# Another hand-written order for the attention groups and the first expert's products of a fused kernel

## The chip, the cores and the metric

The kernel runs on one core of one Trainium2 chip. The metric is device time in microseconds, from launch to end, as a median of runs. The core has five engines with an instruction queue each: PE (matmuls; its weight loads are shown as PEld), DVE (vector), ACT (scalar and activations), POOL (GpSimd) and SP, which here only issues DMA transfers. Each engine works through its queue in order; what must wait for another engine waits on a semaphore, and everything queued behind it on that engine waits too.

## The reference

The program is a chain of three layers over 1152 tokens (2 batches of 576) of 512 features, all in 32-bit floats:

```
scores = q @ k.T / 8, masked (heads 0-3: a band of 32; heads 4-7: every 4th of 128)
attn   = exp(scores - max); attn /= sum(attn) + 1e-9;   x = attn @ v
out    = sum over 4 experts e of  p[:, e] * (relu(x @ w1[e]) @ w2[e])     # 512 -> 1024 -> 512
h      = out @ w_in;  g = h * sigmoid(1.702 * h);  result = g @ w_out     # 512 -> 2048 -> 512
```

Products of full 32-bit precision are made of three passes at a faster format: a number is split into a high part and a rest, and high*high, low*high and high*low are summed in PSUM.

## The kernel before

**Attention.** Only the blocks that the masks leave are computed. Heads go in four pairs; each of the two batches has for each pair a big part and a small part, 16 parts in all. A big part is two *groups*, a small part one, so there are 24 groups, numbered 0 to 23 in the order of the list `parts`: 0, 1 are pair 2 of batch 0; 2, 3 pair 3; 4, 5 pair 0; 6, 7 pair 1; 8 to 15 are the small parts of both batches; 16 to 23 the big parts of batch 1. Pairs 2 and 3 have the dilated mask and four tiles of scores to a group, pairs 0 and 1 the plain band and three (small groups three or four).

The steps of one group x have letters in the table that sets their order:

- `S x` the matmuls for the scores (PE; `S x y` takes two groups in turns), into one PSUM bank;
- `Q x` adds the mask and takes each row's minimum of the negated scores (DVE, one instruction per tile);
- then either `A x`, exponentials tile by tile, with the row's minimum as bias and the row sum as by-product (ACT), or `B x`, a subtraction of the minima from the whole group (POOL `p` or DVE `v`), `X x`, one exponential over the whole group (ACT), and `Y x`, the row sums (DVE);
- `N x` adds 1e-9 and takes the reciprocal (both DVE), then multiplies the group by it (POOL `p` or DVE `v`);
- `U x` transposes the group (PE, into a PSUM bank), `c x` copies it to SBUF (ACT `a`, DVE `v`);
- `V x` multiplies by the values once both groups of a part are there (PE, one bank); `C x` copies the result as the high part of the layer's input `xh`, `R x` forms the rest `xl` (DVE) and frees the bank.

**The first expert, expert 0.** Its tokens go in three chunks c of 384 and its hidden features in eight tiles f of 128. A first product (chunk c, tile f) is 12 matmuls: four slices of the input (one for each head pair) times three passes. Step `F it a b` does some of them for it = 8c + f: the terms a to b-1 of eight, of which 0 to 3 are the two passes with `xh` of slice 0 to 3, and 4 to 7 the one with `xl`. `G f i` does the same for chunk 0, tile f and slice `ORDER[i]`. `h it` (ACT, relu) and `l it` (DVE) read the bank and form the high and low part of the hidden tile; four such buffers go round. `2 it i` is the second product, three matmuls into the i-th of four long-lived banks; after tile 7 DVE multiplies each by the token's share and puts it into `acc`. `W s which` loads a weight slab of 512 KB into one of four staging buffers, `H` (ACT) and `O` (POOL or DVE) split it.

**Banks.** PSUM has eight banks here: four of the pool `ps`, which scores, transposes, value products and first products all take, and four of `pacc` for the second products (chunk 0's first products of tiles 0 to 2 borrow three of those before their time).

**What sets the order.** Up to chunk 1 the table `SCRIPT` is the program order of all five queues: a line of it is read step by step, and each step appends its instructions to its engines. Loads are steps of it too (`L` for q and k of a part, `K` for v, `W`), so it also sets the order of the transfers, all of them in one queue on SP. `P n` puts n matmuls on the constant 1.0 (`spin`), whose results nobody reads. Everything after the table (chunk 2, experts 1 to 3, the last layer) is written by other code:

```
for words_ in SCRIPT.split(","):
    what, *args_ = words_.split()
    steps[what](*(int(x) if x.lstrip("-").isdigit() else x for x in args_))
```

In names of rows, `s02big` is the bank of scores of batch 0, pair 2, big part; `prob`, `st` its exponentials and minima/sums, `ppt` and `pT` the transposed group in PSUM and SBUF, `pv` the value product, `g` (with expert, chunk and tile behind it) a first product, `pa` a second product, `h` the hidden tile, `st_`, `wh`, `wl` a staged slab and its two parts.

Of the kernel before, what the change touches and what calls it, by code (L numbers as in the profile page):

```python
# [76 lines left out]
F 0 7 8, H 1 0 1, Q 8, R 5, O 1 0 v 2, L 10, W 2 0, K 6, D, A 8, K 7, O 1 0 p 1, N 8 p, G 0 2 h, G 1 1 l, U 8, c 7 a,
Q 9, A 9, K 8, W 3 0, L 11, H 0 1 0, c 8 v, N 9 v, V 7, S 10, F 1 0 1, G 1 1 h, F 0 6 7, F 0 0 1, U 9, F 0 2 3, Q 10,
C 7 a, A 10, H 0 1 1, R 7, O 1 0 v 0, F 0 3 6, F 1 6 7, F 0 1 2, N 10 v, H 1 1 0, h 0, c 9 v, O 0 1 v 0, V 8, S 11,
C 8 v, S 12, F 1 7 8, V 9, F 1 3 4, F 1 2 3, Q 11, Q 12, A 12, A 11, l 0, O 0 1 v 1, F 1 5 6, R 8, F 1 4 5, O 1 0 p 3,  # L80
F 2 1 6, U 10, N 12 v, 2 0 0, F 2 0 1, F 1 1 2, O 0 1 v 2, c 10 a, K 9, L 12, L 13, K 10, N 11 p, U 11, H 1 1 1, h 1,
C 9 a, F 2 6 8, c 11 v, O 0 1 v 3, U 12, V 10, V 11, h 2, R 9, l 1, S 13, c 12 v, H 2 0 0, S 14, C 11 a, V 12, l 2,
R 11, O 2 0 p 0, Q 13, Q 14, H 3 0 0, C 12 a, 2 0 1, F 3 7 8, 2 1 0, 2 0 2, F 3 6 7, F 3 5 6, F 3 1 2, F 3 2 5, 2 0 3,
F 3 0 1, 2 1 1, H 2 0 1, A 14, C 10 a, R 12, O 1 1 p 1, O 1 1 v 0, O 2 0 p 1, O 2 0 p 2, A 13, K 11, W 3 1, W 2 1,
L 14, K 12, N 14 v, O 1 1 p 2, O 2 0 p 3, R 10, h 3, N 13 v, l 3, U 14, U 13, c 14 a, c 13 v, H 3 0 1, F 4 2 8, 2 1 2,
2 1 3, F 4 0 1, F 4 1 2, S 15, V 14, h 4, V 13, C 14 a, H 3 1 0, H 2 1 0, H 2 1 1, R 14, C 13 v, R 13, O 3 0 p 1,
O 1 1 v 3, O 3 0 p 2, O 2 1 p 2, O 2 1 p 3, Q 15, 2 2 0, H 3 1 1, B 15 v, X 15, Y 15, F 5 0 2, 2 2 1, 2 3 0, F 5 2 5,
F 5 5 8, 2 3 1, 2 2 2, 2 3 2, 2 2 3, O 3 0 p 3, l 4, N 15 v, h 5, K 13, O 2 1 v 1, l 5, O 3 1 p 2, O 3 0 p 0, L 15,
U 15, F 6 4 6, F 6 2 4, F 6 6 8, 2 3 3, F 6 0 2, w, c 15 a, V 15, h 6, S 16 17, l 6, Q 17, Q 16, C 15 a, B 16 v, R 15,
X 16, Y 16, O 2 1 p 0, O 3 1 p 0, O 3 1 p 1, B 17 v, X 17, Y 17, F 7 7 8, F 7 3 4, 2 4 0, F 7 2 3, F 7 5 6, F 7 6 7,  # L90
F 7 1 2, F 7 0 1, 2 4 1, 2 4 2, 2 5 0, 2 5 1, F 7 4 5, 2 5 2, h 7, Z, F 8 6 7, F 8 0 1, 2 4 3, F 8 1 2, N 16 p,
N 17 p, 2 6 0, U 16, F 8 2 6, K 14, 2 5 3, F 8 7 8, U 17, l 7, c 16 a, c 17 a, S 18 19, V 17, Q 19, Q 18, A 18,
C 17 a, h 8, R 17, A 19, N 18 p, l 8, 2 6 1, O 3 1 v 3, 2 7 0, F 10 0 6, F 9 2 8, 2 6 2, F 9 0 1, U 18, 2 6 3,
F 9 1 2, K 15, N 19 p, c 18 a, h 9, 2 7 1, U 19, 2 8 0, l 9, F 10 6 8, 2 7 2, h 10, c 19 a, 2 7 3, S 20, Q 20, S 21,
V 19, l 10, Q 21, C 19 v, F 11 5 6, F 11 0 4, 2 9 0, F 11 7 8, F 11 4 5, 2 8 1, F 11 6 7, B 20 v, R 19, B 21 p, X 21,
Y 21, h 11, X 20, Y 20, N 21 p, 2 8 2, 2 9 1, 2 9 2, 2 8 3, F 12 0 3, N 20 v, l 11, F 12 6 7, F 12 7 8, U 20, 2 10 0,
# [9 lines left out]
def fused_kernel(ctx: ExitStack, tc: tile.TileContext, qk, v, dp, w1, w2, w_in, w_out, out):  # L106
# [958 lines left out]
    def due(kind, s, c):  # L1065

        one = 7 + len(TILES[1 - c])
        if kind == "1":
# [86 lines left out]
```

## Time and profile before

| | us |
|---|---|
| median of 3 runs (lowest, highest) | 631.91 (631.45, 633.77) |
| the profiled execution: time | 631.46 |
| the profiled execution: span from first to last instruction | 629.7 |
| PE busy, share of the span | 619.1, 98% |
| DVE, POOL, ACT busy | 475.1, 355.3, 276.3 |

The page has a line for each engine (busy time, share, instructions), the span in 40 slices, the DMA queues, the chain of work that ended last, and the costliest groups of instructions. Views of the trace used below: busy time by stretch, who waited for whom, the instructions in order of time, and groups of instructions by line and shape. The time of an execution is 1.76 us longer than its span here.

### The profile page before, as it was taken

Reading aid. Unit: us, or ns where it says so; the run is one execution under the profiler, and the core shown is the slowest. Engines: PE = TensorE matmul, PEld = TensorE weight load, DVE = VectorE, ACT = ScalarE, POOL = GpSimd, SP = SyncE. Lnnn points to the kernel's source line nnn. Section 1 sums busy time; section 2 is a strip of 40 time slices with the busy share of each in tenths; the row PEclk is TensorE's granted clock in tenths of the full one; section 3 lists DMA queues with packets and bytes.
Section 4 is the critical chain, followed back from the end, with each engine's and each line's share of the span. In section 5 each row is a group of like instructions: output and inputs, shape, how many; then the busy total and the mean of one; then the engine's idle time right before and its main releaser. Section 6 shows DMA issues by size and latency. Waiting matters only on the chain.

```text
span 629.7 us, 11219 instructions
## 1 busy us (share of the span) xinstructions
PE 619.1 (98%) x4201; PEld 575.3 (91%) x4202; DVE 475.1 (75%) x1008; ACT 276.3 (44%) x606; POOL 355.3 (56%) x334
## 2 busy tenths in 40 slices
PE   7899999999999999999999999999999999999997
PEld 4689999999999999999999999989898998998996
DVE  3885564495988888888888879999987767667565
ACT  6763422135444444444443543536645344344321
POOL 5234111377578788688688685569336563563310
PEclk9999999999999999999999999999999999999999
DMA  8752420104165346354365364221202211100003
GB/s 275 215 189 99 139 72 4 37 0 137 44 205 161 113 163 189 114 171 138 119 178 171 122 182 118 84 84 67 68 2 68 67 42 61 34 0 1 1 1 150
DMA packets 23174, 64.33 MB, mean 102 GB/s; under 512 B 2764, under 2 KB 4336, under 8 KB 23120
## 3 DMA queue, kind: packets, MB, share of 16 engines
q1 hardware_dynamic: 23120, 63.62, 32.3%
q8 instruction: 33, 0.54, 0.4%
q14 instruction: 21, 0.17, 0.1%
HBM read 52.84 MB, written 10.77 MB: 101 GB/s over the span
## 4 chain that ended last, share of the span: by engine, by line
PE 92%; DVE 4%; ACT 2%; issue 1%; POOL 0%; POOLq 0%; ACTq 0%; DVEq 0%
PE gd L760 10%; PE gc L760 9%; PE ga L760 9%; PE q L864 8%; PE q L866 8%; PE q L865 8%; PE g L492 7%; PE q L894 5%; PE q L892 5%; PE q L893 5%; PE gb L760 5%; PE pa L526 3%; PE pa L528 3%; PE pa L527 3%; PE spin L417 1%
## 5 line engine op out<-in xcount | busy, mean ns | idle before, releaser
L864 PE MATMUL q<-h,w2h 128*128 128x320 f32 (+1 forms) x288 | 97.3, 338 | 0.0
L866 PE MATMUL q<-h,w2h 128*128 128x320 f32 (+1 forms) x288 | 97.2, 337 | 0.0
L865 PE MATMUL q<-h,w2l 128*128 128x320 f32 (+1 forms) x288 | 97.2, 337 | 0.0
L807 DVE TENSOR_TENSOR h<-cc,h 128x256 fp32r<-128x256 f32 (+1 forms) x80 | 73.8, 922 | 20.0 <-ACT h L797 12.5
L703 POOL TENSOR_TENSOR m<-m,sd 128x512 int32<-128x512 int32 x32 | 49.1, 1533 | 62.1 <-ACT h L797 37.2
L874 DVE TENSOR_TENSOR acc<-q,acc 128x512 f32<-128x512 f32 (+1 forms) x132 | 70.6, 548 | 10.8 <-PE q L866 9.5
L647 POOL TENSOR_TENSOR wsl<-ss,wsh 128x512 fp32r<-128x512 f32 x39 | 59.4, 1529 | 31.0 <-ACT wsh L646 20.6
L797 ACT ACTIVATE h<-cc 128x256 fp32r<-128x256 f32 (+3 forms) x48 | 32.9, 686 | 95.9 <-DVE cc L794 95.4
L782 POOL TENSOR_TENSOR cc<-s,u 128x256 f32<-128x256 f32 (+1 forms) x38 | 33.2, 875 | 60.0 <-DVE s L779 59.9
L658 POOL TENSOR_TENSOR w2l<-st,w2h 128x512 fp32r<-128x512 f32 x37 | 55.0, 1499 | 5.6 <-ACT w2h L657 5.2
L866 PEld LDWEIGHTS q<-h,w2h 128*128 128x128 f32 x288 | 54.1, 188 | 4.4
L865 PEld LDWEIGHTS q<-h,w2l 128*128 128x128 f32 x288 | 54.1, 188 | 3.9
L864 PEld LDWEIGHTS q<-h,w2h 128*128 128x128 f32 x288 | 54.1, 188 | 3.8
L894 PE MATMUL q<-w2h,h 128*128 128x512 f32 (+1 forms) x146 | 57.0, 390 | 0.0
L892 PE MATMUL q<-w2h,h 128*128 128x512 f32 (+1 forms) x146 | 56.6, 388 | 0.0
L893 PE MATMUL q<-w2l,h 128*128 128x512 f32 (+1 forms) x146 | 56.6, 388 | 0.0
L901 DVE SCALAR_TENSOR_TENSOR acc<-q,acc 128x512 f32<-128x512 f32 (+1 forms) x64 | 42.6, 678 | 11.6 <-PE q L894 11.3
L643 POOL TENSOR_TENSOR wal<-st,wah 128x512 fp32r<-128x512 f32 (+1 forms) x38 | 46.1, 1219 | 2.3 <-ACT wah L642 2.3
L760 PE MATMUL ga<-xh,wal 128*128 128x256 f32 (+1 forms) x160 | 47.3, 296 | 0.0
L760 PE MATMUL ga<-xl,wah 128*128 128x256 f32 (+1 forms) x160 | 47.3, 295 | 0.0
L760 PE MATMUL ga<-xh,wah 128*128 128x256 f32 (+1 forms) x160 | 47.2, 295 | 0.0
L794 DVE SCALAR_TENSOR_TENSOR cc<-cc,pb 128x256 f32<-128x256 f32 (+3 forms) x48 | 42.4, 883 | 1.0
(387 smaller groups left out, 1739.4 us busy)
## 6 DMA issues: line engine op xcount, KB each, us to landing
st<-in_w_dram SPq DMA_DIRECT2D x32, 512.0 KB, 4.8
sd<-in_w_in_dram SPq DMA_DIRECT2D x16, 512.0 KB, 3.8
sd<-in_w_out_dram SPq DMA_DIRECT2D x16, 512.0 KB, 3.8
w<-m SPq DMA_DIRECT2D x32, 256.0 KB, 4.1
st<-w SPq DMA_DIRECT2D x16, 512.0 KB, 3.5
out_dram<-acc SPq DMA_DIRECT2D x8, 256.0 KB, 2.0
pb<-pd SPq DMA_DIRECT2D x3, 320.0 KB, 3.2
pb<-pd SPq DMA_DIRECT2D x3, 256.0 KB, 4.1
```

The costliest lines, as they stand in the source:

```text
L647: fns.append(lambda x=x, dst=dst: engine(f"p.{s}.{x}").tensor_tensor(out=sl[:, dst], in0=sums[:, dst], in1=sh[:, dst].bitcast(F32), op=ALU ...
L658: fns.append(lambda o=o: engine(f"q.{s}.{2 * o + 1}").tensor_tensor(out=lo[:, o], in0=t[:, o], in1=hi[:, o].bitcast(F32), op=ALU.subtract))
L703: nc.gpsimd.tensor_tensor(out=m.bitcast(I32), in0=m.bitcast(I32), in1=t.bitcast(I32)[:, :, 0], op=ALU.add)
L760: nc.tensor.matmul(bank_[:, :n], wz[:, y, m, :], xz, start=start and m == 0 and z == 0, stop=m == 1 and z == 2, skip_group_check=not start)
L807: nc.vector.tensor_tensor(out=hl[:, sub], in0=cc[:, sub], in1=hh[:, sub].bitcast(F32), op=ALU.subtract)
L864: nc.tensor.matmul(pt, wh[:, o, cols], hi, start=first, stop=False, skip_group_check=both)
L865: nc.tensor.matmul(pt, wl[:, o, cols], hi, start=False, stop=False, skip_group_check=both)
L866: nc.tensor.matmul(pt, wh[:, o, cols], lo, start=False, stop=last, skip_group_check=both)
L874: nc.vector.tensor_tensor(out=dst[:, on], in0=pt[:, on], in1=src[:, on], op=ALU.add)
L892: nc.tensor.matmul(pt, hi, wh[:, o, cols], start=o == 0, stop=False)
L893: nc.tensor.matmul(pt, hi, wl[:, o, cols], start=False, stop=False)
L894: nc.tensor.matmul(pt, lo, wh[:, o, cols], start=False, stop=o == 1)
```

## The change

`SCRIPT` is replaced as a whole; both tables hold the same attention groups and the same products, except for what follows. The groups begin with pair 3 and pair 1 instead of pair 2 and pair 3, and the loads stand in another order, the first weight slab sixth instead of fourth. `P` appears once, with 8 matmuls, where it had 15 in eight places. Groups 6, 7 and 22, 23 get their scores in turns. Eight groups instead of six take their exponentials whole (`B`, `X`, `Y`). 21 of the 24 multiplications `N` go to POOL, where it was 12; of the 32 pieces of `O` 17 stand on POOL, where it was 22. Single terms of many first products stand between the attention steps, and first products of chunk 1 (it 8 and up) begin while second products of chunk 0 are still to come. For that, open products and hidden tiles are kept under (chunk, tile) and no longer under the tile alone. The table's first and last lines, and the rest of the diff without repetitions:

```diff
 SCRIPT = """
-P 6, P 1, L 0, M, L 1, L 2, W 0 0, L 3, K 0, P 1, P 1, P 2, S 0 1, Q 0, A 0, Q 1, W 0 1, L 4, L 5, K 1, K 2, L 6,
...
-R 23, 2 13 3, l 15
+M, L 1, P 8, S 2 3, L 3, Q 3, A 3, S 6 7, Q 6, L 2, Q 2, B 6 p, S 4, L 0, S 0 1, N 3 p, Q 4, A 2, L 5, Q 7, N 2 p,
...
+h 14, 2 12 0, F 15 4 5, 2 12 1, h 15, l 14, V 23, V 19, l 15, 2 13 1, C 19 a, C 23 v, R 21, R 19, 2 13 3, 2 13 0, R 23
 """
...
-        if f not in part:
+        if (c, f) not in part:
             early_bank = e == 0 and c == 0 and f < NTI
             pool, tag = (pacc, f"pa{KT - 1 - f}") if early_bank else (ps, "ps")
-            part[f] = [pool.tile([P, 512], F32, tag=tag, name=f"g1_{e}{c}{f}"),
+            part[c, f] = [pool.tile([P, 512], F32, tag=tag, name=f"g1_{e}{c}{f}"),
...
-        hbuf[f] = hp.tile([P, 2, C], F32R, tag="h", name=f"h{e}{c}{f}")
+        hbuf[c, f] = hp.tile([P, 2, C], F32R, tag="h", name=f"h{e}{c}{f}")
...
-    def second(s0, f, name, tiles):
+    def second(s0, c, f, name, tiles):
...
-            t = hbuf[f]
+            t = hbuf[c, f]
...
-        if tiles[-1] == KT - 1:
-            hbuf.pop(f)
```

On PE, the place of the first transposes. Ahead of these rows stand, before, eleven spin matmuls and the scores of groups 0 to 3; now eight spin matmuls and the scores of groups 2, 3, 6, 7, 4, 0 and 1. Before:

```order
L417 MATMUL spin<-const-bfloat16-1.0 128x512
L344 MATMUL ppt02big_263<-ident,prob02big_202 96x96 x4
L300 MATMUL s00big_268<-qkT00big 64x96 x6
L300 MATMUL s00big_275<-qkT00big 64x96 x6
L417 LDWEIGHTS const-bfloat16-1.0
```

Now:

```order
L303 MATMUL s02big_239<-qkT02big 96x96
L347 MATMUL ppt03big_270<-ident,prob03big_191 96x96 x4
L347 MATMUL ppt03big_282<-ident,prob03big_222 96x96 x4
L303 MATMUL s00big_287<-qkT00big 64x96 x6
L347 MATMUL ppt01big_325<-ident,prob01big_215 96x128 x3
```

Seven groups' scores stand ahead of the first transpose where there were four, and no spin matmul stands behind it.

On POOL, the first rows behind the masks. Before:

```order
L336 TENSOR_TENSOR prob02big_202<-prob02big_202,st02big_203 96x4x96
L336 TENSOR_TENSOR prob02big_212<-prob02big_212,st02big_213 96x4x96
L205 TENSOR_TENSOR wl_0_250<-st_0_182,wh_0_249 128x256
L336 TENSOR_TENSOR prob03big_252<-prob03big_252,st03big_253 96x4x96
L205 TENSOR_TENSOR wl_0_250<-st_0_182,wh_0_249 128x256
L336 TENSOR_TENSOR prob03big_287<-prob03big_287,st03big_288 96x4x96
```

Now (L322 is `B`, the subtraction for group 6; L339 is `N`):

```order
L322 TENSOR_TENSOR prob01big_215<-prob01big_215,st01big_216 128x3x96
L339 TENSOR_TENSOR prob03big_191<-prob03big_191,st03big_192 96x4x96
L339 TENSOR_TENSOR prob03big_222<-prob03big_222,st03big_223 96x4x96
L339 TENSOR_TENSOR prob01big_215<-prob01big_215,st01big_216 128x3x96
L339 TENSOR_TENSOR prob01big_262<-prob01big_262,st01big_263 128x3x96
L208 TENSOR_TENSOR wl_0_297<-st_0_294,wh_0_296 128x256 x3
```

The subtraction and four multiplications stand ahead of the first weight pieces, which stood between them.

On PE, the place where several products of chunk 1 (`g_01` and the tile's number) are open. Before, tile 0 and the next to open, tile 2, stand apart, and tile 2's terms in a row:

```order
L492 MATMUL g_012_1202<-xh,wl_1_444 128x384
L492 MATMUL g_012_1202<-xl,wh_1_443 128x384 x2
L492 MATMUL g_011_1213<-xh,wh_0_249 128x384
L492 MATMUL g_011_1213<-xh,wl_0_250 128x384
L492 MATMUL g_011_1213<-xh,wh_0_249 128x384
```

Now, with the last term of tile 0 at the top and the first of tile 1 at the foot:

```order
L495 MATMUL g_010_1173<-xl,wh_0_296 128x384
L495 MATMUL g_012_1215<-xh,wh_1_431 128x384
L495 MATMUL g_012_1215<-xh,wl_1_432 128x384
L495 MATMUL g_012_1215<-xl,wh_1_431 128x384
L529 MATMUL pa_00_741<-h_1059,wh_2_863 128x384
L530 MATMUL pa_00_741<-h_1059,wl_2_864 128x384
L531 MATMUL pa_00_741<-h_1059,wh_2_863 128x384
L495 MATMUL g_013_1217<-xl,wh_1_431 128x384
...
L495 MATMUL g_012_1215<-xl,wh_1_431 128x384
L495 MATMUL g_015_1235<-xl,wh_2_624 128x384
L495 MATMUL g_011_1248<-xh,wh_0_296 128x384
```

Tiles 0, 2, 3 and 5 of chunk 1 hold all four `ps` banks there, and tile 1 takes the bank that tile 0 leaves; 14 matmuls stand between the two.

## Rows read from the trace of the kernel before

**Rows 1.** The page, part 1: busy us (share of span) x instructions.

```profile
PE 619.1 (98%) x4201; PEld 575.3 (91%) x4202; DVE 475.1 (75%) x1008; ACT 276.3 (44%) x606; POOL 355.3 (56%) x334
```

**Rows 2.** Busy time by stretch: stretch, length, engines, PE clock granted, DMA share, GB/s.

```profile
0.00:10.00 10.00, 6.95 (x44) 3.24 (x44) 2.54 (x26) 4.12 (x17) 5.77 (x26) 1.00 0.77 265
10.00:20.00 10.00, 8.16 (x97) 6.03 (x100) 7.39 (x44) 8.61 (x41) 5.30 (x8) 1.00 1.04 313
20.00:40.00 20.00, 18.17 (x261) 15.51 (x263) 15.54 (x82) 14.96 (x60) 3.96 (x6) 1.00 0.73 204
...
40.00:112.00 72.00, 71.94 (x603) 68.11 (x599) 39.72 (x154) 24.24 (x74) 20.71 (x27) 1.00 0.27 87
```

**Rows 3.** Who PE waited for, 0 to 112 us, the largest: total, times, longest.

```profile
PE ppt02big L344 <- POOL prob02big L336: 2.4, 1, 2.4
```

**Rows 4.** PE in order of time (start, us), and the first scores' duration (ns min/median/max).

```profile
0.76 4.85 PE L417 MATMUL spin<-const-bfloat16-1.0 128*128 128x512 bf16 x11 [0.76 <-PEq L1140]
5.55 1.17 PE L300 MATMUL s02big<-qkT02big 64*96 64x96 f32 x16
6.55 0.84 PE L300 MATMUL s03big<-qkT03big 64*96 64x96 f32 x16
...
10.14 0.54 PE L344 MATMUL ppt02big<-ident,prob02big 96*96 96x96 f32 x4 [2.42 <-POOL prob02big L336]
10.61 1.21 PE L300 MATMUL s00big<-qkT00big 64*64 64x96 f32 x24
...
L300 PE MATMUL s02big<-qkT02big x16: 244/245/473, 5.5 to 6.5; 64*96 64x96 f32 x16
```

**Rows 5.** Groups by line and shape, 0 to 112 us: xcount | busy us, mean ns | idle before.

```profile
L417 PE MATMUL spin<-const-bfloat16-1.0 128*128 128x512 bf16 x14 | 6.0, 575 | 0.9 <-PEq L1140 0.8 <-issue 0.2
L313 ACT ACTIVATE prob02big<-prob02big,st02big 96x96 f32<-96x96 f32 x8 | 2.9, 361 | 5.2 <-DVE st02big L308 5.2
L308 DVE CUSTOM_DVE_ANT_0 prob02big<-s02big,mA 96x96 f32<-96x96 f32 x8 | 1.5, 249 | 6.9 <-PE s02big L300 6.9
L336 POOL TENSOR_TENSOR prob02big<-prob02big,st02big 96x384 f32<-96x384 f32 x2 | 1.6, 822 | 3.1 <-DVE st03big L308 3.1
L324 ACT ACTIVATE prob10big<-prob10big 128x288 f32<-128x288 f32 x2 | 0.9, 441 | 3.3 <-POOL prob10big L319 3.3
L328 DVE TENSOR_REDUCE st10big<-prob10big 128x3 f32<-128x288 f32 x2 | 0.9, 446 | 2.0 <-ACT prob10big L324 2.0
L502 ACT ACTIVATE h<-g 128x384 fp32r<-128x384 f32 x15 | 7.3, 485 | 16.9 <-PE g L492 16.9
L506 DVE SCALAR_TENSOR_TENSOR h<-g,h 128x384 fp32r<-128x384 f32 x15 | 8.2, 546 | 1.9 <-ACT h L502 1.9
```

**Rows 6.** Transfers: issues on SP (start, us), then sizes and us from issue to landing.

```profile
0.72 0.39 SPq L241 DMA_DIRECT2D qkT02big<-in_qk_dram  x1
1.64 0.42 SPq L241 DMA_DIRECT2D qkT00big<-in_qk_dram  x1
2.58 0.43 SPq L241 DMA_DIRECT2D qkT01big<-in_qk_dram  x1
...
qkT02big<-in_qk_dram SPq DMA_DIRECT2D x1, 384.0 KB, 3.3
qkT00big<-in_qk_dram SPq DMA_DIRECT2D x1, 384.0 KB, 5.1
qkT01big<-in_qk_dram SPq DMA_DIRECT2D x1, 384.0 KB, 7.5
```

**Rows 7.** DVE and POOL in order of time: start, us.

```profile
42.67 3.05 POOL L205 TENSOR_TENSOR wl<-st,wh 128x256 fp32r<-128x256 f32 x4 [1.10 <-ACT wh L197]
...
44.37 0.74 DVE L336 TENSOR_TENSOR prob10small<-prob10small,st10small 128x288 f32<-128x288 f32 x1
45.99 0.46 DVE L336 TENSOR_TENSOR prob01small<-prob01small,st01small 128x288 f32<-128x288 f32 x1
```

**Rows 8.** The chain that ended last, in order of time: one first product of chunk 2.

```profile
133.98 2.09 PE g L492 x12
```

More of the change, by code (lines that the diff above doesn't have):

```diff
@@ L77 @@
[L77 to L96, printed above, removed]
@@ new lines @@
+K 8, V 5, Q 8, C 1 a, O 1 0 p 2, N 10 p, S 13, Q 12, R 1, X 14, S 11, C 5 a, S 15, K 9, Y 14, W 0 1, R 5, O 0 0 v 2,
+A 12, N 14 p, B 9 p, F 2 0 1, H 2 0 0, U 10, c 10 a, N 12 p, H 2 0 1, O 2 0 v 0, G 0 0 l, F 1 6 7, F 1 2 3, G 0 2 h,
+F 0 4 5, G 0 0 h, U 14, F 2 2 3, F 2 7 8, U 12, F 2 4 5, W 3 0, F 4 5 6, L 12, Q 11, F 1 0 1, X 9, h 0, O 2 0 p 1,
+F 1 4 5, A 11, O 2 0 v 2, O 2 0 v 3, c 14 v, H 0 1 0, Q 15, F 4 6 7, O 0 1 p 0, c 12 v, H 0 1 1, O 0 1 p 3, F 3 5 6,
+Q 13, Y 9, h 1, H 3 0 0, F 4 2 3, V 10, V 12, B 8 v, l 0, F 3 1 2, X 8, F 3 3 4, l 1, 2 0 0, L 14, B 13 p, B 15 p,
@@ new lines @@
+Y 8, X 13, O 0 1 p 1, F 3 6 7, Y 13, F 3 4 5, N 8 p, F 2 6 7, F 4 7 8, X 15, h 2, F 4 1 2, Y 15, F 3 7 8, K 11, K 7,
+N 11 p, C 10 a, N 9 p, F 4 0 1, F 4 3 4, F 4 4 5, C 12 v, 2 0 1, K 4, W 2 1, R 10, W 1 1, 2 0 3, O 0 1 p 2, U 11,
+H 3 0 1, F 3 2 3, R 12, h 4, F 3 0 1, l 2, U 8, 2 0 2, D, l 4, O 3 0 p 1, c 11 v, h 3, O 3 0 v 0, c 8 v, S 16 17, U 9,
+N 13 p, l 3, 2 1 1, Q 17, H 1 1 0, H 2 1 0, O 1 1 p 1, 2 1 3, H 1 1 1, 2 1 0, S 21, V 11, c 9 a, Q 16, V 9, V 8,
+O 1 1 v 0, Q 21, V 14, 2 2 0, 2 2 1, F 7 4 5, 2 1 2, H 2 1 1, O 2 1 p 1, O 1 1 v 2, O 3 0 v 2, F 6 1 2, C 9 v,
@@ new lines @@
+F 7 7 8, F 5 4 5, A 21, W 3 1, H 3 1 0, O 3 0 p 3, C 8 a, F 7 6 7, R 9, F 6 6 7, 2 2 3, F 5 6 7, F 5 2 3, C 11 a,
+F 7 1 2, R 8, F 7 2 3, L 15, F 7 3 4, N 15 p, F 7 5 6, H 3 1 1, F 7 0 1, F 5 3 4, F 5 1 2, F 6 0 1, 2 2 2, U 13,
+2 3 1, R 11, U 15, A 16, O 1 1 v 3, 2 3 3, O 2 1 p 0, O 2 1 v 3, h 7, C 14 a, N 16 p, F 5 5 6, 2 3 2, 2 3 0, l 7,
+F 5 7 8, F 6 3 4, N 21 p, A 17, U 21, R 14, c 13 a, N 17 v, F 6 5 6, w, c 15 v, F 5 0 1, h 5, L 13, c 21 a, l 5,
+F 6 7 8, 2 4 2, O 3 1 p 0, O 3 1 p 1, F 6 2 3, F 6 4 5, h 6, 2 4 3, U 16, 2 4 0, 2 4 1, S 18 19, c 16 a, l 6,
@@ new lines @@
+O 2 1 v 2, Z, 2 5 2, 2 6 2, V 13, V 15, S 22 23, S 20, Q 18, Q 19, C 13 v, R 13, 2 5 3, O 3 1 v 3, F 8 7 8, F 8 4 5,
+Q 22, C 15 a, F 8 1 2, K 15, U 17, R 15, F 8 3 4, 2 6 3, F 8 0 1, Q 23, 2 5 1, F 8 2 3, Q 20, F 8 6 7, F 10 6 7,
+F 11 4 5, F 8 5 6, F 10 3 4, F 10 4 5, A 19, A 18, 2 5 0, F 11 7 8, F 13 0 1, F 11 3 4, B 22 p, F 13 7 8, X 22,
+F 10 5 6, Y 22, F 13 5 6, h 8, F 9 1 2, F 9 4 5, B 23 p, c 17 v, X 23, Y 23, F 13 3 4, K 12, F 13 4 5, F 9 0 1, 2 6 1,
+l 8, F 9 6 7, F 9 2 3, O 3 1 p 2, 2 7 2, 2 7 1, F 11 6 7, F 13 1 2, F 13 6 7, 2 6 0, F 13 2 3, F 9 3 4, h 13,
@@ L102 @@
+F 15 0 1, c 22 v, F 14 5 6, F 15 3 4, F 14 4 5, U 18, 2 11 2, 2 12 3, 2 12 2, c 18 a, C 21 a, 2 13 2, U 23, c 23 a,
+h 14, 2 12 0, F 15 4 5, 2 12 1, h 15, l 14, V 23, V 19, l 15, 2 13 1, C 19 a, C 23 v, R 21, R 19, 2 13 3, 2 13 0, R 23
 """
@@ L474, in g1_part @@
     def g1_part(e, c, f, kt, terms):
-        if f not in part:
+        if (c, f) not in part:
             early_bank = e == 0 and c == 0 and f < NTI
             pool, tag = (pacc, f"pa{KT - 1 - f}") if early_bank else (ps, "ps")
-            part[f] = [pool.tile([P, 512], F32, tag=tag, name=f"g1_{e}{c}{f}"),
+            part[c, f] = [pool.tile([P, 512], F32, tag=tag, name=f"g1_{e}{c}{f}"),
                        {(k, x) for k in range(KT) for x in "hl"}]
-        pt, todo = part[f]
+        pt, todo = part[c, f]
         s, o = divmod(f, 2)
@@ L499, in g1_upper @@
     def g1_upper(e, c, f):
-        assert not part[f][1]
-        hbuf[f] = hp.tile([P, 2, C], F32R, tag="h", name=f"h{e}{c}{f}")
-        nc.scalar.activation(hbuf[f][:, 0, :], part[f][0][:, :C], AF.Relu)
+        assert not part[c, f][1]
+        hbuf[c, f] = hp.tile([P, 2, C], F32R, tag="h", name=f"h{e}{c}{f}")
+        nc.scalar.activation(hbuf[c, f][:, 0, :], part[c, f][0][:, :C], AF.Relu)
     def g1_lower(e, c, f):
-        pt, _ = part.pop(f)
-        nc.vector.scalar_tensor_tensor(hbuf[f][:, 1, :], pt[:, :C], 0.0, hbuf[f][:, 0, :].bitcast(F32),
+        pt, _ = part.pop((c, f))
+        nc.vector.scalar_tensor_tensor(hbuf[c, f][:, 1, :], pt[:, :C], 0.0, hbuf[c, f][:, 0, :].bitcast(F32),
                                        op0=ALU.max, op1=ALU.subtract)
@@ L534, in g2 @@
             pbe[c] = load_p(pb0, e, c * C, (c + 1) * C, "pb0")
-        second(4 * e, f, f"_{e}{c}", tiles)
+        second(4 * e, c, f, f"_{e}{c}", tiles)
         if f == F1 - 1:
```

18 lines of the change are left out of this document (10 added, 8 removed).

## Prediction

> **What bounds the kernel now.** The first view is the busy time of each engine: PE works 619.1 of the span's 629.7 us [rows 1], so the whole can shrink only by what PE doesn't do, about 10.6 us, and by matmuls that are no work. The second is busy time by stretch: PE is idle for 3.05 us of the first 10, 1.84 of the next 10 and 1.83 of the next 20, together 6.72 us; from 40 to 112 us, just past the table's end, it lacks 0.06 of 72 [rows 2]. The spin matmuls, whose results nobody reads, take another 6.0 us, 4.85 of them in one row ahead of the first scores [rows 4, 5]. So 12.7 us up to 40 us are no work. The longest idle piece, 2.42 us, is the first transpose waiting for a multiplication on POOL [rows 3, 4]. There the kernel is bound by the chain from the first load through scores, minima, exponentials and multiplication; behind it by PE. Behind the table the code is unchanged, so what the table gains at its end stays.
>
> **The change part by part.** I add up what PE will spend on no work in the new order, by following the queues with durations of rows.
>
> *Spin matmuls, first load.* One costs 4.85/11 = 0.44 us [rows 4]; eight from 0.76 on end at 4.3. The first load is now pair 3, also 384 KB; pair 2's was issued at 0.72 and landed 3.3 later, at 4.0 [rows 6]. So scores begin at 4.3 in place of 5.55, and 4.3 us are no work.
>
> *Half clock.* The granted clock column shows full speed throughout [rows 2], but the first score matmuls last 473 ns and later ones 244 [rows 4], the ratio of 1.2 to 2.4 GHz. Sixteen take 1.17 us at first and 0.84 right behind [rows 4]: 0.33 us lost, so the lower level covered 0.66 us of scores and ended near 6.2. If it ends at 6.2 again, it covers 1.9 us and costs 0.95: 0.6 more than before.
>
> *The scores' end and the fourth load.* Groups 2, 3 cost about 0.8 us, 6, 7 and 4 some 1.2 and 0.6 (24 matmuls, 1.21) [rows 4]; with the 0.95 group 4 ends at 7.8. Its load, the third, should land at 6.7 as pair 0's did (1.64 + 5.1); the second, landing between, is in time for 6, 7 at about 5.9. Groups 0 and 1 need the fourth. Between 6.7 and the landing of pair 1 at 10.1 there came 512 and 384 KB [rows 6], so 384 KB are about 1.4 us: it lands at 8.1 to 8.2. Wait: 0.4 us.
>
> *First transposes, U 3 and U 2.* Exponentials of group 3 start by 6.2 and end by 7.65 (four of 0.36). DVE still has the minima of 6 and 2 ahead of N 3 (seven at 1.5/8 = 0.19 us) and comes to it at about 8.5; its two small instructions take 0.37, POOL 0.82: ready at 9.85 [rows 5]. POOL's subtraction for group 6 (about 0.67) is over by then. PE ends the scores of 0 and 1 at 8.95: wait 0.9. U 2 comes through N 2, behind the minima of 4 and 7 and the same 0.37 + 0.82, at 11.3, where PE is free at 10.35: wait 0.95. So the 2.42 us at the first transpose become two waits of 1.85 together, but 0.3 us earlier and with seven groups' scores done where there were four. Shorter waits to 27 us: 0.15.
>
> The sum of no work is 4.3 + 0.6 + 2.4 = 7.3 us in place of 12.7: a gain of 5.4. My following of queues errs on the side of too few waits; I take off 0.7, one more wait of a POOL multiplication's size (0.82). **Gain 4.7 us.**
>
> *More on POOL.* Nine more multiplications go there. One takes 0.82 where DVE took 0.46 [rows 5, 7], so 0.36 is added to the latency of that group, and DVE is relieved of 9 x 0.46 = 4.1 us. What POOL gives up is five pieces of weights, which DVE takes. Beside a running POOL instruction DVE's multiplication took 0.74 in place of 0.46 [rows 7], 0.28 more. DVE is busy 25.5 of the first 40 us [rows 2]: room enough as a mean, not at each place; that is in the 0.7.
>
> *Whole exponentials.* Two groups more: three exponentials on ACT (1.08 us) become one (0.44), DVE gets the sums (0.45), POOL a subtraction [rows 5]. All lies beside PE's work, off the path unless a chain is late. Turns of groups 22, 23 and the changed keys cost nothing: as many matmuls, no instruction.
>
> *Loads.* The first weight slab is sixth. With 512 KB at the same pace behind the fifth load it lands at about 11.2, and ACT, which splits it, comes to it at about 11.5: a margin of 0.3 that costs nothing here, and 1.0 us at most if the loads slip by one slab's queue place. Other loads stand a microsecond or more ahead of their users.
>
> *From 28 us to the end of the table.* Both orders hold the same matmuls, and in the old one PE waits hardly at all there, so nothing can be gained; only lost. Each first product needs a bank. The tightest place is where tile 1 of chunk 1 takes tile 0's bank, which is free only after h (0.49) and l (0.55) [rows 5]; ahead of l on DVE and h on ACT stand an exponential and its sums (0.44, 0.45): with the passing from engine to engine about 2.4 us. The 14 matmuls between last cover 14 x 0.17 = 2.4 [rows 8]. Price nothing, without reserve; other places I followed have 0.35 us or more.
>
> **Bounds.** If all waits are hidden, the gain is 5.4 + 2.4 = 7.8 us. If waits sum up to what is idle between the spins and 40 us before (6.72 less the 0.76 at the start, 5.96), no work is 4.3 + 0.6 + 5.96 = 10.9 and the gain 1.8.
>
> The profiled execution took 631.46; less 4.7 is 626.8. The median of the runs lies 0.45 above it: **627.2 us**.
>
> **The rivals.** (A) *The chain stays the bound and the waits as long.* Gain 1.8, so about 630.1. For it: the chain has the same steps, the multiplication is on POOL in nine more groups, and DVE is slowed beside it; nine times 0.28 are 2.5 us, and if each also stops a transpose for its 0.36 of latency, 3.2 more, where 2.9 would do. Against: first products are strewn between, so PE has work from other rows while a multiplication runs. The Trainium skill (SBUF — State Buffer, "Who interferes with whom") says that a DVE instruction with both inputs in SBUF contends with a GpSimd one that reads SBUF, and calls the port pair an exclusive lock, whose loser fully blocks; by that each meeting could cost up to POOL's whole 0.82, 7.4 us for nine, and with all of them bare on the path the time would be 631.9 − 4.7 + 7.4 = 634.6. By the trace the rule agrees in kind and not in size: 0.28 beside 0.82 [rows 7]. Chance 0.15.
>
> (B) *Open products of chunk 1 hold the banks.* Four `ps` banks are taken by tiles of chunk 1 while transposes, value products and the next tile want one. If at each of seven takings h, l and a quarter of a microsecond between engines stand bare, 0.49 + 0.55 + 0.25 = 1.3 us [rows 5], PE loses 9.1, and the time is 631.9 − 4.7 + 9.1 = 636.3, slower than before. It decides when fewer than about eight matmuls (1.3/0.17) stand between a tile's last term and the next user of its bank. The order shows 14 at the tightest place I found, so 0.08.
>
> (C) *The half clock lasts.* With three fewer spins and pauses at 7.8, 8.95 and 10.35 the higher level may come only near 12 us. The 5.8 us from 6.2 hold 2.25 of waits and 3.5 of work; doubled, they cost 3.5 less what the waits take in (about 1.5): 2.0, so 629.2. Against: before, PE stood idle for 2.42 us ahead of 10.14, and the 24 matmuls at 10.61 took 1.21 [rows 4], the higher level. The Trainium skill (TensorE: Matmul & The Clock Gate, Part 1) has the array start at half clock, activity releases it and idleness brings it back; by that the shorter spin row speaks for this rival, the row at 10.61 against it. Chance 0.06.
>
> (D) *The waits all hide*: 631.9 − 7.8 = 624.1, if DVE reaches N 3 a microsecond earlier than I have it. Chance 0.08.
>
> **How the numbers follow.** The forecast, 625.5 to 628.8, has 0.63; A 0.15, B 0.08, C 0.06, D 0.08. A measurement of this kernel can tell about 0.5% from no change, 3.2 us: faster is below 628.75, slower above 635.1. Faster: the forecast, D, less some of its upper edge, 0.68. Same: A, C and that edge, 0.24. Slower: B, 0.08. The range leaves out B and half of D and takes in A and C with some slack: 624.5 to 631.0.
>
> **What would show it.** First scores at 4.3; the first transpose of pair 3 near 9.85 with POOL as releaser; PE idle in the first 40 us 3.2 to 3.9 us, the start's 0.76 among them, where it was 6.72; nothing idle from 60 us on; score matmuls of 473 ns until about 6.2; the first matmul of chunk 2 between 4 and 5.5 us earlier than in the kernel before. Wrong it would be if idle pieces of over a microsecond stood behind first products of chunk 1, or matmuls of twice the time after 7 us.

## The result

The changed kernel takes 623.99 us (median of 4 runs, 623.73 to 625.40), the kernel before 631.85 (4 runs): a ratio of 0.9874, with a 95% interval from 0.9849 to 0.9899. Five more runs gave 623.18 to 623.81; the median of all nine is 623.76, and differences below are taken against it. The gain is 7.9 us where 4.7 was forecast, and the time lies 0.5 us below the range.

The profiled execution took 623.73, its span is 621.9 where it was 629.7. Part 1 of the page of the changed kernel, to set beside [rows 1]:

```profile
PE 613.7 (99%) x4195; PEld 573.7 (92%) x4195; DVE 471.8 (76%) x1002; ACT 275.1 (44%) x597; POOL 360.8 (58%) x343
```

PE is busy for 5.4 us less, and 2.4 us less idle. Busy time by stretch, as [rows 2] (length, PE, PEld, DVE, ACT, POOL, PE clock granted, DMA share, GB/s):

```profile
0.00:10.00 10.00, 7.57 (x80) 4.55 (x80) 4.28 (x40) 5.58 (x23) 7.06 (x28) 1.00 0.82 273
10.00:20.00 10.00, 9.25 (x150) 8.10 (x152) 8.85 (x62) 9.68 (x43) 6.75 (x10) 1.00 1.05 271
20.00:40.00 20.00, 18.81 (x212) 17.12 (x209) 17.39 (x76) 12.45 (x39) 12.45 (x17) 1.00 0.81 252
40.00:105.00 65.00, 65.00 (x567) 62.40 (x566) 31.66 (x125) 23.54 (x79) 13.01 (x19) 1.00 0.24 80
```

Up to 40 us PE is idle for 2.43 + 0.75 + 1.19 = 4.37 us, where it was 6.72. Behind 40 us it is never idle. The order of PE's rows (start, duration, what, and in brackets the idle time before them and what ended it), as [rows 4]:

```profile
0.76 3.23 PE L420 MATMUL spin<-const-bfloat16-1.0 128*128 128x512 bf16 x8 [0.76 <-PEq L1141]
4.12 0.92 PE L303 MATMUL s03big<-qkT03big 64*96 64x96 f32 x16
5.05 1.26 PE L303 MATMUL s01big<-qkT01big 64*64 64x96 f32 x24
6.87 0.71 PE L303 MATMUL s00big<-qkT00big 64*64 64x96 f32 x12 [0.56 <-DMA qkT00big<-in_qk_dram]
7.95 0.92 PE L303 MATMUL s02big<-qkT02big 64*96 64x96 f32 x16 [0.37 <-DVE st03big L337]
9.06 0.54 PE L347 MATMUL ppt03big<-ident,prob03big 96*96 96x96 f32 x4 [0.19 <-POOL prob03big L339]
10.39 0.54 PE L347 MATMUL ppt03big<-ident,prob03big 96*96 96x96 f32 x4 [0.79 <-POOL prob03big L339]
```

Scores begin at 4.1, the first transpose stands at 9.06 and waits 0.19 us, the second 0.79. The waits of PE up to 105 us, the largest (total, times, longest):

```profile
PE pv02big L373 <- DVE st13small L311: 1.1, 1, 1.1
PE ppt03big L347 <- POOL prob03big L339: 1.0, 2, 0.8
PE spin L420 <- PEq L1141: 0.8, 1, 0.8
PE s00big L303 <- DMA qkT00big<-in_qk_dram: 0.6, 1, 0.6
```

**Where the 7.8 us of the span come from.** The first matmul of expert 1 (`ga`) is a fixed point, since the code behind the table is the same. Before, then in the changed kernel:

```profile
150.55 0.28 PE L760 MATMUL ga<-xh,wah 128*128 128x256 f32 x1
```

```profile
142.72 0.28 PE L761 MATMUL ga<-xh,wah 128*128 128x256 f32 x1
```

It comes 7.83 us earlier, all of the gain. (The first matmul of chunk 2 comes 7.8 us earlier too, at 105.07 and not 112.88, where 4 to 5.5 were forecast.) Up to it I added up PE's matmuls one by one, each from its start to the next one's start with the idle time taken out, by kind; the counts are equal but for the spins:

| us up to expert 1 | before | changed | difference |
|---|---|---|---|
| spin matmuls | 5.77 | 3.23 | −2.54 |
| idle, without the start's 0.76 | 6.01 | 3.60 | −2.41 |
| scores | 13.69 | 13.38 | −0.31 |
| transposes | 8.19 | 7.75 | −0.44 |
| value products | 11.34 | 9.89 | −1.45 |
| first products | 53.17 | 52.30 | −0.87 |
| second products | 51.59 | 51.77 | +0.18 |

Spins and idle time give 4.95 us, close to the forecast of 4.7. (The kernel before has 15 spin matmuls in its table; its trace shows 14.) But the same 1204 matmuls of the five lower rows took 137.98 us and take 135.09. These 2.89 us were in no term of the sum.

### The profile page after: what moved, and what is told of

It is laid out like the page before. It is cut to its first block, busy times and chain, and to the rows that moved or that the text cites. A ratio compares the mean times of both kernels' runs of the same rounds, so it can differ in the third digit from the quotient of the medians.

```text
span 621.9 us, 11212 instructions
## 1 busy us (share of the span) xinstructions
PE 613.7 (99%) x4195; PEld 573.7 (92%) x4195; DVE 471.8 (76%) x1002; ACT 275.1 (44%) x597; POOL 360.8 (58%) x343
## 4 chain that ended last, share of the span: by engine, by line
PE 93%; DVE 3%; DMA 3%; ACT 1%; issue 0%; SPq 0%; ACTq 0%; DVEq 0%
PE gd L761 10%; PE gc L761 10%; PE ga L761 10%; PE q L865 8%; PE q L866 8%; PE q L867 8%; PE g L495 7%; PE q L895 5%; PE q L893 5%; PE q L894 5%; PE gb L761 5%; PE pa L529 3%; PE pa L531 3%; PE pa L530 3%; DMA qkT10small<-in_qk_dram 2%; DMA qkT03small<-in_qk_dram 1%
```

## The experiments

The theory that I formed on the table (S): PE pays for every change between attention matmuls and product matmuls, and the new order has fewer. A *visit* is a run of scores and value products (with transposes among them) between matmuls of other kinds: products, spins, and the one transpose of the tokens' shares (`p_t`). PE makes 16 visits before and 10 now, with 22 and 13 changes of kind inside them. Two of the 16 are only set apart by spins; between products alone there are 14 and 10. Its rival (H): all is made in the head, and the order of kinds is free.

### More visits, nothing else: apart

```diff
-2 1 1, Q 17, H 1 1 0, H 2 1 0, O 1 1 p 1, 2 1 3, H 1 1 1, 2 1 0, S 21, V 11, c 9 a, Q 16, V 9, V 8,
-O 1 1 v 0, Q 21, V 14, 2 2 0, 2 2 1, F 7 4 5, 2 1 2,
+Q 17, H 1 1 0, H 2 1 0, O 1 1 p 1, H 1 1 1, S 21, 2 1 1, V 11, 2 1 3, c 9 a, Q 16, V 9, 2 1 0, V 8, 2 1 2,
+O 1 1 v 0, Q 21, V 14, 2 2 0, 2 2 1, F 7 4 5,
...
-Z, 2 5 2, 2 6 2, V 13, V 15, S 22 23, S 20, Q 18, Q 19, C 13 v, R 13, 2 5 3,
+Z, V 13, 2 5 2, V 15, 2 6 2, S 22 23, 2 5 3, S 20, Q 18, Q 19, C 13 v, R 13,
```

and in the same way `F 4 2 3` between V 10 and V 12, `F 14 2 3` between V 21 and V 17, `2 13 1` between V 23 and V 19.

> The changed kernel with ten product steps of three or four matmuls moved between attention steps that stood in a row on PE (value products and scores of groups 9, 10, 12, 13 to 15, 17 to 23, all behind 30 us, where PE has no idle time); the same matmuls, in all twenty more changes of kind on PE. In the two traces a change between scores or value products and something else takes about 0.12 us more than the matmuls themselves, and the kernel before has some thirteen more of them. Theory S (changes of kind on PE are paid, and fewer of them are the part of the gain that the sum missed): 1.8 to 2.4 us slower than the changed kernel, 625.8 to 626.4, with the loss spread over these ten places. Rival H (the whole gain is made in the head, by waits and spins, changes of kind are free): within 0.3 us of the changed kernel.

Measured: 627.11 us (626.61 to 627.26), 3.35 slower than the changed kernel; by the spans 3.25 (625.1). The visits are 19, counted in the trace, nine more (18 between products alone). The changed kernel's rows at the first place of the diff above:

```profile
42.97 0.71 PE L303 MATMUL s10big<-qkT10big 64*64 64x96 f32 x12
43.62 0.57 PE L373 MATMUL pv00small<-pT00small,v00small 96*64 96x64 f32 x12
44.02 0.62 PE L373 MATMUL pv03small<-pT03small,v03small 80*64 80x48 f32 x16
44.47 0.64 PE L373 MATMUL pv02small<-pT02small,v02small 80*64 80x48 f32 x16
44.94 0.53 PE L373 MATMUL pv10small<-pT10small,v10small 96*64 96x64 f32 x12
45.40 0.44 PE L529 MATMUL pa<-h,wh 128*128 128x384 f32 x1
45.68 0.34 PE L530 MATMUL pa<-h,wl 128*128 128x384 f32 x1
45.85 0.34 PE L531 MATMUL pa<-h,wh 128*128 128x384 f32 x1
```

and of apart:

```profile
42.53 0.44 PE L530 MATMUL pa<-h,wh 128*128 128x384 f32 x1
42.81 0.33 PE L531 MATMUL pa<-h,wl 128*128 128x384 f32 x1
42.98 0.34 PE L532 MATMUL pa<-h,wh 128*128 128x384 f32 x1
43.25 0.57 PE L374 MATMUL pv00small<-pT00small,v00small 96*64 96x64 f32 x12
43.75 0.45 PE L530 MATMUL pa<-h,wh 128*128 128x384 f32 x1
44.03 0.33 PE L531 MATMUL pa<-h,wl 128*128 128x384 f32 x1
44.20 0.34 PE L532 MATMUL pa<-h,wh 128*128 128x384 f32 x1
44.47 0.67 PE L374 MATMUL pv03small<-pT03small,v03small 80*64 80x48 f32 x16
```

Read the distances between starts. In a row of products one follows the other after 0.17 us. The first product behind an attention matmul takes 0.28 (42.53 to 42.81), the last one ahead of one 0.27 (42.98 to 43.25), and `pv00small` holds PE for 0.50 (43.25 to 43.75) where ahead of another value product it held it for 0.40 (43.62 to 44.02). That is 0.11 + 0.10 + 0.10 = 0.3 us per visit, and no row calls it idle. The weight loads show where a part of it arises:

```profile
42.64 0.19 PEld L531 LDWEIGHTS pa<-h,wl 128*128 128x128 f32 x1
42.81 0.19 PEld L532 LDWEIGHTS pa<-h,wh 128*128 128x128 f32 x1
43.25 0.43 PEld L374 LDWEIGHTS pv00small<-pT00small,v00small 96*64 96x64 f32 x12 [0.25 <-issue]
43.75 0.19 PEld L530 LDWEIGHTS pa<-h,wh 128*128 128x128 f32 x1
43.85 0.19 PEld L531 LDWEIGHTS pa<-h,wl 128*128 128x128 f32 x1
```

Among products a weight load starts up to 0.17 us ahead of its own matmul (42.64 for the one at 42.81). At the change of kind load and matmul start together, at 43.25 and at 43.75, and ahead of 43.25 the loader is idle for 0.25 us. The five kinds sum up to 137.98 us in apart, 2.89 more than in the changed kernel (by chance the sum of the kernel before); 0.18 more stands at the transpose of the shares (`p_t`), which now has a value product behind it, and 0.2 in the head. So 0.32 us per visit: that changes of kind are paid holds, at a price half as high again as I expected, since I had left out the first product behind a visit. H falls. How much of the 2.89 us between the two kernels this explains is another question, and comes below.

### The spins and the start: spin11, spin0, before_spin8, before_start8

In the changed kernel `P 8` becomes `P 11`:

```diff
-M, L 1, P 8, S 2 3,
+M, L 1, P 11, S 2 3,
```

> The changed kernel with 11 spin matmuls at the start instead of 8, as the kernel before has them. If each is paid at 0.43 us (theory: the spin row sets the start): first scores at 5.4, 1.3 us slower, 625.2. Rival (loads set the pace: groups 4, 0 and 1 wait 0.56 us for their loads in the changed kernel, and the clock was up from 3.5 us on, so that the three cost 0.22 each): first scores at 4.7, at most 0.3 us slower.

Measured: 624.31 (623.85 to 625.97), 0.55 us slower. But the median mixes two things. The two runs with a mean clock of 0.999 took 623.85 and 623.89, 0.1 us slower, as the rival says; the two at 0.997 and 0.995 took 624.73 and 625.97. In the profiled one, at 0.997, scores begin at 5.17, 1.05 us later, the wait for pair 0's load is gone, and the first transpose stands at 10.04; its clock then fell (0.94 granted from 8 to 12 us, 0.63 from 12 to 16). So the rival holds: with the clock up, the waits behind take in the three spins nearly whole.

Without the spins:

```diff
-M, L 1, P 8, S 2 3,
+M, L 1, S 2 3,
```

> The changed kernel without any spin matmul. PE waits for the first load, which landed at 4.1 us, so scores start no earlier than 4.1. Theory (the spins only wake the clock): scores at twice their duration until the clock rises, 1 to 2 us more work, less what the waits for loads take in: 0.5 to 1.5 us slower, 624.4 to 625.4. Rival (the clock rises as early without them, or the first chain is bound by loads and DVE anyway): within 0.3 us.

Measured: 624.34 (624.00 to 624.65): 0.6 slower, the lower end of the theory. Scores begin at 3.78, when the load lands (I had expected 4.1), at the slower duration:

```profile
L304 PE MATMUL s03big<-qkT03big x16: 364/364/470, 3.8 to 5.0; 64*96 64x96 f32 x16
```

In the kernel before, all three later places of `P` (four matmuls) removed and 8 spins left at the start:

```diff
-P 6, P 1, L 0, M, L 1, L 2, W 0 0, L 3, K 0, P 1, P 1, P 2, S 0 1,
+P 8, L 0, M, L 1, L 2, W 0 0, L 3, K 0, S 0 1,
...
-A 1, S 2 3, N 0 p, H 0 0 0, Q 2, A 2, P 1, U 0,
+A 1, S 2 3, N 0 p, H 0 0 0, Q 2, A 2, U 0,
```

> The kernel before with its 14 spin matmuls cut to 8 in one row at the start, the rest of its table unchanged. Theory (only the spins ahead of the first scores are on the path, the others stand in waits of the chain): 1.3 us faster than the kernel before, 630.6. If all spins were paid: 2.5 us, 629.4. Rival (the clock or the loads take it back): within 0.3 us of the kernel before.

Measured: median 632.39 of 10 runs, from 629.62 to 633.35, beside 631.32 for the kernel before. The fastest run, the profiled one, is 1.4 us faster than the median of the kernel before at full clock (631.03, 20 runs), as the theory wants. But it is one of only two with the clock granted in full, and the other took 631.8; in the eight others the mean over the span was 0.989 to 0.997, and they took 631.5 to 633.4. Five of the ten stand at 0.989, a value that the kernel before has in none of 37 runs (0.994 is its lowest). So the spins that went were worth something that the trace of before does not show. The last of this group keeps the later ones, and drops three of the early ones:

```diff
-P 6, P 1, L 0, M, L 1,
+P 3, P 1, L 0, M, L 1,
```

> The kernel before with 8 spin matmuls instead of 11 ahead of the first scores, and the four later ones kept where they are. In before_spin8, which dropped those too, the one run at full clock was 1.5 us faster than the kernel before, and most others were slower, with the clock at 0.989 to 0.997. Theory (the three early spins are paid, the later ones hold the clock up in the pauses at 8 to 13 us): at full clock 1.3 us faster, 629.8, and runs below full clock no more frequent than in the kernel before (about four in ten). Rival (the clock falls for want of the early spins): as slow and scattered as before_spin8, median near 632.

Measured: median 630.46 of 12 runs (629.55 to 633.23), before 631.15. With the clock in full (six runs) 629.55 to 630.11, 1.1 us faster; below it in six of twelve, where the kernel before had seven of 17, and never below 0.994. The theory holds: early spins are paid nearly one to one in the kernel before (1.1 us for three of 0.44), and with the later ones in place the falls to 0.989 are gone. Whether the falls to 0.994 and 0.997 come more often without the early ones, twelve runs can't tell.

### Other parts of the change: n_as_before, tilewise, tilewise_again

Every `N` gets the engine it had before, 12 on each (12 go back to DVE, three to POOL):

```diff
-N 6 p, ... N 4 p, ... N 5 p, ... N 10 p,
+N 6 v, ... N 4 v, ... N 5 v, ... N 10 v,
```

> The changed kernel with every multiplication N on the engine that the kernel before gives it to (12 on DVE, 12 on POOL instead of 3 and 21). The prediction charged POOL's longer multiplication with 0.36 us of latency at each. Theory (DVE is the fuller engine where it counts, 8.85 of the 10 us from 10 to 20): back on DVE the minima and copies behind it come later, 0.5 to 1.5 us slower than the changed kernel, with more PE idle time between 10 and 40 us. Rival (latency of N counts): 0.3 to 1 us faster.

Measured: 625.84 (624.54 to 627.19), 2.1 slower. The rival does not come. But the theory's reason, more idle time of PE, is not what the trace shows: up to expert 1 the profiled execution is idle for 2.56 us (without the start), 1.04 less than the changed kernel, and its matmuls take 2.75 more. Its clock fell, and slower matmuls can fill waits (columns as in [rows 2]):

```profile
14.00:16.00 2.00, 2.00 (x23) 1.41 (x21) 1.30 (x10) 2.00 (x13) 1.91 (x3) 0.50 1.01 370
```

Three of the four runs have a mean clock of 0.995 or 0.997. The one at full clock took 624.54, 0.8 more than the changed kernel's median and less than its slowest run (625.40). So this order of engines is the better one as measured; that this is so at full clock is not shown.

```diff
-B 6 p, ... X 6, A 7, Y 6, ... B 14 p, ... X 14, ... Y 14,
+... A 6, A 7, ... A 14,
```

and so for groups 8, 9 and 13.

> The changed kernel with groups 6, 8, 9, 13 and 14 back to exponentials tile by tile (no subtraction on POOL or DVE, no sums on DVE), at the place where the whole exponential stood. ACT gets about 0.65 us more for each, DVE 0.45 and POOL 0.67 less. Theory (ACT is full from 10 to 20 us, 9.68 of 10, so group 6 whole counts, the others don't): 0.3 to 1 us slower than the changed kernel, lost before 20 us. Rival (nothing waits for ACT there, all of it lies beside PE's work): within 0.2 us.

Measured: 625.08 (623.63 to 626.69). More runs:

> The kernel tilewise once more (five groups back to exponentials tile by tile). Its one run at full clock took 623.6 us, the changed kernel's time; the others were 1.5 to 3 us slower with the clock at 0.994 to 0.997. Theory (the whole exponentials shorten no path at full clock, but the head without them has a pause ahead of 12 us in which the clock falls): runs at full clock at 623.6 to 624.0, and half of the runs or more below 0.998 and above 624.9. Rival (they are worth 1 us at full clock): no run below 624.5.

Measured: 625.41 (624.11 to 625.67). Of ten runs three had the clock at 0.999 or more, and took 623.63, 624.11 and 625.33; the others, at 0.994 to 0.997, 625.07 to 626.69. What the whole exponentials are worth at full clock stays open between 0 and 1.6 us; in the profiled one of the three (625.33) PE is idle for 4.68 us up to expert 1, 1.1 more than in the changed kernel. That without them the clock falls in seven of ten runs is plain; the changed kernel has none of nine.

### The changed kernel again: after_again

> The changed kernel itself, more runs. Several of the other kernels' runs granted less than full clock for some microseconds in the head (0.994 to 0.997 of the span, 2 to 3 us slower), among them a quarter to a half of those of the kernel before. Theory (the changed kernel keeps PE busy enough in the head to keep the clock): at least nine of ten runs at 0.999 or above and within 624 +- 0.7 us. Rival (by chance in the first four runs): as many runs at 0.997 or below as the kernel before has.

Measured: 623.18 to 623.81 (5 runs), all at 0.999 or 1.0, like the four runs of the result (of which one, at 625.40, is above the 0.7 us that I allowed). The theory holds for all nine runs in clock. In time six of nine lie within its 0.7 us of 624, and two, at 623.18 and 623.27, are faster. The clock's first rise still moves about. Durations of the first scores (ns, min/median/max; first and last start) in the two profiled executions of this kernel:

```profile
L303 PE MATMUL s03big<-qkT03big x16: 245/245/320, 4.1 to 4.8; 64*96 64x96 f32 x16
```

```profile
L303 PE MATMUL s03big<-qkT03big x16: 264/364/469, 4.3 to 5.5; 64*96 64x96 f32 x16
```

The second had most of these scores at the slower durations, and its span was 621.7, 0.2 shorter than the first's. What it lost at the start it got back from the waits behind: the value product that waits 1.07 us in the one waits 0.46 in the other.

### Two attempts at a faster version: q_early, joined

```diff
-V 1, c 5 a, O 1 0 v 0, K 8, V 5, Q 8, C 1 a, O 1 0 p 2, N 10 p, S 13, Q 12,
+V 1, c 5 a, Q 8, Q 12, O 1 0 v 0, K 8, V 5, C 1 a, O 1 0 p 2, N 10 p, S 13,
```

> The changed kernel with the minima of groups 8 and 12 moved on DVE ahead of a weight piece (0.41 us) and of group 10's two small instructions (0.37 us). At 21.8 us PE stands idle for 1.07 us, the longest wait of the changed kernel, ended by the second of these. Theory (a wait of PE in the head goes into the time one to one, since behind it PE is never idle): the wait shrinks by up to 0.8 us and the kernel is 0.5 to 0.8 us faster, 623.2 to 623.5. Rival (the next wait takes its place): within 0.2 us.

Measured: 623.78 (623.30 to 624.93), the changed kernel's time. The wait went from 1.07 to 0.37 us:

```profile
PE pv02big L374 <- DVE st13small L312: 0.4, 1, 0.4
```

but in after_again it was 0.46 by itself. Against that execution PE's idle time sums to 2.25 us (without the start) where it was 2.78, and the scores take 14.50 where they took 13.92, more of them at half clock. The two cancel, and what the edit alone is worth can't be told.

On top of that, two visits less:

```diff
-S 16 17, U 9, N 13 p, l 3, 2 1 1, Q 17, ... 2 1 0, S 21, V 11,
+U 9, N 13 p, l 3, 2 1 1, ... 2 1 0, S 16 17, S 21, Q 17, V 11,
...
-Z, 2 5 2, 2 6 2, V 13, V 15, S 22 23, S 20, Q 18,
+Z, V 13, V 15, S 22 23, S 20, 2 5 2, 2 6 2, Q 18,
```

> The changed kernel with the order of q_early and two visits of PE to attention work taken away behind 40 us: the scores of groups 16 and 17 stand just ahead of those of group 21, and two product steps that stood ahead of the value products of groups 13 and 15 stand behind the scores of group 20. In apart, ten visits more cost about 3.0 us, 0.3 each. Theory (a visit is priced the same when it goes): 0.5 to 0.7 us faster than q_early, about 623.2, if the banks come free in time. Rival (scores brought together wait for banks that the minima must free): the same as q_early or slower.

Measured: 625.29 (624.41 to 626.10), 1.5 slower. The rival holds: products took 0.3 us less in sum than in q_early, about the price of one visit (by the trace nine are left of ten, or eight between products alone), but the banks were late, behind the minima:

```profile
PE s11big L304 <- DVE st13big L312: 0.4, 1, 0.4
...
PE pv10small L374 <- DVE st10big L312: 0.3, 1, 0.3
...
PE pv02small L374 <- DVE st12big L312: 0.2, 1, 0.2
```

The idle time is 0.5 us more than in q_early, and the four groups of matmuls around these waits (`s11big`, `pv00small`, `pv02small`, `pv03small`) take 0.96 us more from start to start: waits that look busy.

Nothing that was tried beats the changed kernel.

## Why the prediction fell short

- **What bounds the kernel**: right. Head bound by a chain, the rest by PE; what is gained at the table's end stays to the last microsecond.
- **Head**: right in sum. No work was to fall from 12.7 to 7.3 us with 0.7 of allowance; it fell to 0.76 + 3.23 + 3.60 = 7.6. In detail the waits were 3.6 instead of 2.4, but a clock that had risen by the time the scores began saved the 0.6 of half clock, and the first transpose stood at 9.06 instead of 9.85 (whose terms, 8.5 + 0.37 + 0.82, give 9.69). The one error paid for the other: PE came to group 4 early and stood 0.56 us for its load. PE idle in the first 40 us was 4.37, above the 3.2 to 3.9 that I named. As a term of its own the half clock is doubtful too: in after_again the waits behind took it in, though without any spins (spin0), where most of the first scores ran at it, the kernel was 0.6 us slower.
- **"From 28 us to the end of the table"**, and with it the way the sum was made: this is the step that failed. "In the old one PE waits hardly at all there, so nothing can be gained; only lost" took busy time for work, here and in the head, and so put at nothing what a matmul costs next to one of another kind. The 2.89 us that this left out come, by adding up starts, from: about 1.0 at the borders of visits (matmuls of scores or values ahead of a product 11 before and 7 now, with the slow first product behind each; those behind a product are eight in both, since several visits begin with a transpose, and a transpose behind a product costs nothing); about 0.5 at changes of kind inside visits; about 0.4 at the first matmuls of each run of scores or values, 28 runs before and 20 now; and some 0.5 in the kernel before's half clock and in two early value products that waited within themselves. The rest, about 0.5, I can't place. By apart's 0.32 us for a whole visit, the visits that went are worth 1.9 us if all six are counted and 1.3 between products alone, so the first two items lie between 1.5 and 2.4. That such changes cost is shown by apart; their share is worked out from the two traces and not shown by a run of its own. Pieces of waits that look busy are not among the items, though they exist. One can be read in the kernel before:

```profile
25.25 0.34 PE L492 MATMUL g<-xl,wh 128*128 128x384 f32 x1
27.01 0.63 PE L344 MATMUL ppt02small<-ident,prob02small 128*80 128x128 f32 x4 [1.42 <-POOL prob02small L336]
```

  From start to start these are 1.76 us, and the product needs 0.17 of it when another follows. 1.42 are called idle, so 0.17 of the wait stands under the product's 0.34. Eight matmuls (spins aside) stand ahead of a wait in this way before, and eight now, four of them among the first scores; what they take beyond their like sums up to 1.4 us in either trace.
- **Whole exponentials and more on POOL at no cost**: no run shows a cost. At full clock N is settled by one run alone (0.8 us the other way, within the changed kernel's own spread), and the exponentials are open. What I did not have is that without either the clock falls in most runs.
- **The Trainium skill's lock** ("SBUF — State Buffer", "Who interferes with whom"): I took 0.28 us for the size of a meeting. The changed kernel has a meeting that shows more, DVE and POOL in order of time:

```profile
9.74 0.62 DVE L337 TENSOR_SCALAR st01big<-st01big 128x3 f32<-128x3 f32 x1
```

```profile
9.51 0.82 POOL L339 TENSOR_TENSOR prob03big<-prob03big,st03big 96x384 f32<-96x384 f32 x1 [0.50 <-ACT prob01big L316]
```

The small addition, 0.16 us elsewhere, ends at 10.36, just behind POOL's end at 10.33: there it was blocked for the whole rest, as the Trainium skill says in that section. The six other such additions that lasted over 0.2 us in the two traces, three in each, also end 0.02 to 0.03 behind the POOL instruction they began beside. It cost no forecast gain: with the multiplications back where they were the kernel was slower.
- **Rivals**: A (chain as long as before), B (banks) and C (half clock lasts) did not come. B's mechanism exists, as joined shows with its banks behind the minima. D gave 624.1, and the measured 624.0 is next to it by luck: the waits did not hide, and the rest came from where D has nothing.

## What to carry to other kernels

A PE that is busy all the time is not yet a PE that does nothing but work: take its matmuls from start to start and see what each costs behind another kind. Put steps of one kind side by side as long as their banks and inputs are there; here each run of attention matmuls among products that was added cost 0.3 us, and pulling them closer than the banks allow cost more than it gave. Spins ahead of the first scores cost time one to one only where no later wait takes them in (three were worth 1.1 us in the kernel before and 0.1 in the changed one), and spins in a pause may be what holds the clock. Where the clock can fall, compare runs at the same clock before a median is called an effect.

## What the runs showed of the hardware

**The clock can fall in the head of a kernel, in some executions and not in others.** Of 37 runs of the kernel before beside these experiments, 20 had the clock in full over the span and took 630.7 to 631.4 us, seven had a mean of 0.997 (631.1 to 631.9) and ten 0.994 (633.6 to 633.9). In the profiled execution of tilewise the fall can be seen (length, PE, PEld, DVE, ACT, POOL, PE clock):

```profile
8.00:12.00 4.00, 2.28 (x24) 1.55 (x24) 3.36 (x33) 4.00 (x22) 2.19 (x3) 1.00 1.07 294
12.00:16.00 4.00, 3.90 (x36) 2.79 (x38) 2.23 (x20) 4.00 (x19) 2.88 (x5) 0.58 1.02 321
16.00:20.00 4.00, 4.00 (x59) 3.71 (x60) 2.11 (x6) 1.93 (x9) 0.67 (x1) 0.57 1.07 247
```

and of the changed kernel, where it stayed:

```profile
8.00:12.00 4.00, 3.02 (x41) 2.23 (x41) 3.86 (x33) 4.00 (x17) 2.56 (x4) 1.00 1.06 305
12.00:16.00 4.00, 4.00 (x80) 3.54 (x80) 3.69 (x18) 4.00 (x23) 3.15 (x5) 1.00 1.04 316
```

Ahead of the fall to the lower of the two levels (1.2 GHz) PE was busy for 2.28 of 4 us, in the changed kernel 3.02. That busy time alone decides is not shown: the kernel before's own profiled execution kept its clock.

```profile
8.00:12.00 4.00, 1.70 (x29) 1.49 (x31) 2.42 (x26) 4.00 (x22) 2.14 (x3) 1.00 1.04 339
```

The Trainium skill (TensorE: Matmul & The Clock Gate, Part 1) has the array fall back when it is idle. The runs agree in part: the kernel before, with its longer pauses, falls in 17 of 37 runs, before_spin8 in eight of ten, before_start8 in six of twelve, the changed kernel in none of nine. But in tilewise PE was busy for more than half of the stretch ahead of the fall, and its longest idle piece there was 0.78 us, where the kernel before kept its clock through a piece of 2.42; and spin11, with three spins more, fell in two of four. What decides in a single execution stays open. The profiled executions compared above, of the kernel before and of the changed one, both had the clock in full from 7 us on, so their 7.8 us hold none of this; with a run of before at 633.7 the gain is 10, and from the median of its 20 runs at full clock (631.03) it is 7.3.
